# Weights' sums by ScalarE copies and adding DMAs instead of GpSimd, a triple's tiles four apart, and SBUF additions of a triple in two pairs

## The chip, the cores and the metric

The kernel runs on one core of one Trainium2 chip. The metric is the device time of one execution in microseconds (us); the numbers to compare are medians of several executions. The profile and the trace come from one further, profiled execution. Engines are named as in the profile: PE (TensorE; PEld is its weight load), DVE (VectorE), ACT (ScalarE), POOL (GpSimd), and SP (SyncE, which only issues DMAs here).

## The reference

A linear attention with a decay per channel (4 batches, 8 heads, 768 tokens, 48 channels per head) feeds a bilinear feed-forward layer. The weights arrive as 64-bit floats, everything else as 32-bit floats.

```python
f = 1.0 / (1.0 + np.exp(-f_logit))
for t in range(S):
    state = f[:, :, t, :, None] * state + np.einsum('bhd,bhe->bhde', k[:, :, t], v[:, :, t])
    y[:, :, t] = np.einsum('bhd,bhde->bhe', q[:, :, t], state)
...
x = y.transpose(0, 2, 1, 3).reshape(B * S, H * D)      # 3072 x 384
out = (x @ w_a) * (x @ w_b) @ w_out                    # d_ff 1536, out 3072 x 384
```

## The kernel before

All work is in `by_quotients`. Tokens come in 8 blocks of 384 (`BLK`), two to a batch. The attention of a block is two units of four heads each, so there are 16 units (0 to 15). A unit's work is cut into pieces: `front` (two sigmoids on ACT, L284 and L286, one POOL operation, L288, then on DVE two decay scans at L293, L294, eight scans at L303 and two multiplications by q and k at L305 and L306), `scores` (PE L340, DVE L356), `turn` (transposes on PE L368, an ACT copy L372), `gains` (PE L388, DVE L402, L404 and L411), `within` (PE L422) and `across` (PE L443, ACT copies y at L456, and SP moves y into xT, the transposed input of the feed-forward layer).

The feed-forward layer of a block has two halves, "up" (x times w_a and w_b, and their product) and "down" (times w_out).

- Batch 0 (blocks 0 and 1) uses `up` (L490): for one of twelve column tiles of 128, three matmuls for w_b and three for w_a, then an ACT copy (L505) and a DVE multiplication (L507). While these run, the weights are still being converted from 64-bit pieces (`from_double`: ACT at L54, L55, L58 and L59, POOL at L56, DVE at L64 and L66). The raw pieces lie in four places of a pool called `raw`.
- Batches 1 to 3 (blocks 2 to 7) use `up_triples` (L580 to L661). It multiplies a 3x3 arrangement of weight tiles with a 3x2 arrangement of x tiles by fifteen products of sums instead of eighteen plain products; one triple makes three column tiles for both weights, so a block has four triples and the kernel 24. One product is four matmul records at L586. The products are written in a fixed order into four PSUM banks, called v, u, r and t. ACT copies a bank to SBUF (`first` at L617, `late` at L620, L597 in `finish`), and DVE adds: SBUF to SBUF at L621 after a `late` copy, PSUM to SBUF at L624 (`add`). A product may start when the bank's last reader has finished. `finish` (L595 to L601) does the fifteenth product, v6, of a triple inside the next one, then one DVE multiplication of 1152 elements. A triple yields three times.
- `combine_w_ba` (L516 to L549) makes the sums of the weights that the triples need. It has 26 POOL additions at L543 of 128x512 each. Their results lie in the four places of `raw` and partly in w_ba itself.
- `combine_x` (L551 to L578) makes a block's sums of x with 11 DVE operations at L561. It is called ahead of each of blocks 2 to 7, after part 4 of the `down` before it.
- `down` (L680 to L741) takes a pair of 128-token groups and does seven products (x0, m1, x1, m0, x0, m0, x1) of twelve matmuls at L698 each, in two of the four PSUM banks; x0 and x1 are halves of one bank, m0 and m1 of another. Ahead of them DVE makes the sums s3, s1, s2 and s4 (L693), and behind them u2, u3 and the four quarters of the result (L693 too); ACT copies u2 (L711), u3 (L720) and c11 (L733). There are three `down`s in a batch. `combine_w_out` (L667 to L678) makes their weight sums once, in batch 0.

The order of instructions on each engine is the order in which the program writes them. A main list (`rest`) has the ups, triples and downs; beside them runs a queue of (due step, generator) pairs that `beside()` empties. A step is one `up` or a third of a triple; each of the seven parts of a `down` counts half a step. The slots of attention units stand in this queue with due steps written out by hand, and so does `combine_w_ba`:

```python
for_w = combine_w_ba()
queue += [(15.6 + 0.9 * n, for_w) for n in range(9)] + [(24.2 + 0.9 * n, for_w) for n in range(5)]
```

Of the kernel before, what the change touches and what calls it, by code (L numbers as in the profile page):

```python
# [129 lines left out]
def by_quotients(ctx, tc, q, k, f_logit, v, moe_w_a, moe_w_b, moe_w_out, out, ident, weights, bad):  # L130
# [20 lines left out]
    raw_pool = ctx.enter_context(tc.tile_pool(name="raw", bufs=4))  # L151
# [29 lines left out]
    last = groups[:, NTG + 1:2 * NTG].rearrange("p g c -> p (g c)")  # L181
    x_sums = fixed([128, 5 * (BLK // 2)], "x_sums")
    b_copies = itertools.cycle([x_sums[:, BLK * i:BLK * i + BLK] for i in range(2)])
    tails = fixed([128, NU], "tails")
    held = fixed([128, NU, 2], "held")

# [35 lines left out]
    def load_weights(n=1):  # L222
        for _ in range(n):
            if len(raws) == len(todo):
                return
            dst, src, (k, m) = todo[len(raws)]
            raw = dst
            if src.dtype != FP32:

                if len(raws) in EARLY:  # L230
                    raw = groups[:, EARLY.index(len(raws))].bitcast(mybir.dt.uint64)
                else:
                    raw = raw_pool.tile([128, PIECE], mybir.dt.uint64, tag="raw", name="raw")
# [281 lines left out]

    def combine_w_ba():  # L516

        halves = []
        for _ in range(4):
            raw = raw_pool.tile([128, PIECE], mybir.dt.uint64, tag="raw", name="raw").bitcast(FP32)  # L520
            halves += [raw[:, 512 * i:512 * i + 512].rearrange("p (j c) -> p j c", c=128) for i in range(3)]
        s = [halves[2 * i:2 * i + 2] for i in range(6)]
        (a11, a12, a13), (a21, a22, a23), (a31, a32, a33) = (
            [[w_ba[:, g, k].rearrange("p (j i c) -> p i j c", i=NI, c=128)[:, i] for g in range(2)] for k in range(NKT)]
            for i in range(NI)
        )
        for to, x, y, op in (
            (s[0], a21, a32, ALU.add),
            (s[1], a12, a22, ALU.add),
            (s[2], s[1], a21, ALU.add),  # L530
            (s[1], s[1], a23, ALU.add),
            (s[3], a12, s[1], ALU.subtract),
            (s[3], s[3], a32, ALU.subtract),
            (s[4], a31, a11, ALU.subtract),
            (s[5], s[4], a32, ALU.add),
            (s[4], a33, s[4], ALU.subtract),
            (a22, s[1], s[4], ALU.subtract),
            (a22, a22, a13, ALU.add),
            (a31, a31, a33, ALU.subtract),
            (a31, a31, a21, ALU.add),  # L540
        ):
            for g in range(2):
                nc.gpsimd.tensor_tensor(to[g], x[g], y[g], op)  # L543
            yield
        sums_of_w.update(
            v1=s[0], v2=a32, v3=s[3], v4=s[1], v5=a12, v6=s[2],
            u1=a21, u2=a31, u3=s[4], u4=a11, u5=s[5],
            t1=a22, t2=a13, r2=a23, r3=a33,
        )  # L549

    def combine_x(blk):  # L551

        x = xT[blk].rearrange("p k (i t) -> p k i t", i=2)
        (b11, b12), (b21, b22), (b31, b32) = ([x[:, k, i] for i in range(2)] for k in range(NKT))
        s = x_sums.rearrange("p (n t) -> p n t", t=HT)
        more = last[:, 2 * NI * BLK:].rearrange("p (n t) -> p n t", t=HT)
        u5, u3, v6, v1, u1 = (s[:, n] for n in range(5))
        v2, v4, t2, r2 = (more[:, n] for n in range(4))

        def op(to, x, y, op):  # L560
            nc.vector.tensor_tensor(to, x, y, op)  # L561
# [12 lines left out]
        sums_of_x[blk] = dict(  # L574
            v1=v1, v2=v2, v3=b22, v4=v4, v5=b21, v6=v6,
            u1=u1, u2=b12, u3=u3, u4=b11, u5=u5,
            t1=b31, t2=t2, r2=r2, r3=b32,
        )  # L578

    def up_triples(blk):  # L580
# [3 lines left out]
        def times(ps, name, j, start=False):  # L584
            for g in range(2):
                nc.tensor.matmul(  # L586
                    ps[:, g],
                    lhsT=sums_of_w[name][g][:, j],
                    rhs=sums_of_x[blk][name],
                    start=start and g == 0,  # L590
                    stop=True,
# [3 lines left out]
        def finish(j, c, out, v):  # L595
# [2 lines left out]
            a, b = (  # L598
                c[:, g].rearrange("p k i t -> p k (i t)").rearrange("p k (g t) -> p g k t", g=NTG) for g in range(2)
            )  # L600
            nc.vector.tensor_tensor(to[:, :, NI * j:NI * j + NI], a, b, ALU.mult)  # L601

        for j in range(NJ3):
            v, u, r, t = (ps_f[i][:, 0:BLK].rearrange("p (g t) -> p g t", g=2) for i in free)
            free[:] = [free[i] for i in (2, 3, 1, 0)]
            c = (sums, last[:, 0:2 * NI * BLK])[j % 2].rearrange("p (g k i t) -> p g k i t", g=2, k=NI, i=2)
            out = {(k, i): c[:, :, k, i] for k in range(NI) for i in range(2)}
            if j % 2:
                at = (thirds.index(down_first[0]) + 1) * 2
                places = [(at + n) % 6 for n in range(4)]  # L610
                spaces = sums
            else:
                places, spaces = range(4), last
            temps = [spaces[:, BLK * n:BLK * n + BLK].rearrange("p (g t) -> p g t", g=2) for n in places]

            def first(k, i, ps):
                nc.scalar.copy(out[k, i], ps)  # L617

            def late(k, i, ps, temp):
                nc.scalar.copy(temp, ps)  # L620
                nc.vector.tensor_tensor(out[k, i], out[k, i], temp, ALU.add)  # L621

            def add(k, i, ps):
                nc.vector.tensor_tensor(out[k, i], ps, out[k, i], ALU.add)  # L624

            times(v, "v1", j, True)
            first(2, 0, v)
            if tail:
                finish(*tail)
            times(u, "u1", j, True)  # L630
            first(1, 1, u)
            times(r, "r2", j, True)
            add(1, 1, r)
            times(v, "v2", j)
            first(2, 1, v)
# [12 lines left out]
            late(0, 1, v, temps[1])  # L648
            yield
            times(u, "u4", j)  # L650
            late(0, 0, u, temps[2])
            times(t, "t2", j)
            add(0, 1, t)
            times(v, "v5", j)
            late(0, 0, v, temps[3])
            times(u, "u5", j)
            add(2, 0, u)
            tail = j, c, out, v
            if j == NJ3 - 1:
                finish(*tail)  # L660
# [3 lines left out]
    combos = []  # L664
    down_first = [thirds[0]]

    def combine_w_out():  # L667

        b11, b12, b21, b22 = (
            w_out[:, HFT * i:HFT * i + HFT, HM * j:HM * j + HM] for i in range(2) for j in range(2)  # L670
        )
        combos.extend(spare.rearrange("p (i k m) -> i p k m", i=3, k=HFT))
        t1, t2, t4 = combos
        combos.insert(2, b12)
        nc.vector.tensor_tensor(t1, b12, b11, ALU.subtract)
# [3 lines left out]

    def down(pair):  # L680

        b11, b21, b22 = (w_out[:, HFT * i:HFT * i + HFT, HM * j:HM * j + HM] for i, j in ((0, 0), (1, 0), (1, 1)))
        t1, t2, t3, t4 = combos
        (blk0, g0), (blk1, g1) = pair
        a11, a12 = (products(blk0)[:, g0, HFT * i:HFT * i + HFT] for i in range(2))
        a21, a22 = (products(blk1)[:, g1, HFT * i:HFT * i + HFT] for i in range(2))

        def block():
            down_first[0] = thirds[(thirds.index(down_first[0]) + 1) % 3]
            return thirds[thirds.index(down_first[0]) - 1].rearrange("p (k t) -> p k t", k=HFT)  # L690

        def add(to, x, y, op=ALU.add):
            nc.vector.tensor_tensor(to, x, y, op)  # L693
# [2 lines left out]
        def times(to, x, w, first=False):  # L696
            for i in range(HFT):
                nc.tensor.matmul(  # L698
                    to, lhsT=x[:, i], rhs=w[:, i], start=first and i == 0, stop=i == HFT - 1, skip_group_check=True
                )  # L700

        s3 = add(block(), a21, a11, ALU.subtract)
# [89 lines left out]
    with tc.manual_schedule():  # L792
# [540 lines left out]
```

## Time and profile before

| | before |
|---|---|
| median of 3 executions | 634.61 us (632.54 to 634.79) |
| the profiled execution: time | 633.08 us |
| its span in the profile | 631.0 us |
| mean granted PE clock | 0.975 |
| PE busy | 577.4 us (91%) |
| DVE busy | 432.0 us (68%) |
| ACT busy | 276.4 us (44%) |
| POOL busy | 106.0 us (17%) |

The span is what the profile covers; the execution's own time is 2.1 us longer. Busy rows of the page are shares in forty equal slices of the span, 15.8 us each, as a digit in tenths. In the timeline a row is start, duration, engine, line, operation, tiles, and in brackets how long the engine was idle before and what released it. A row of the waits is the waiting instruction, the one waited for, and the total, the number and the longest wait.

The phases of the span are: up to 146 us loading, weight conversion, the attention units of batch 0 and the 24 `up`s; 146 to 219 us the three `down`s of batch 0 with attention units of batch 1; from 219 us blocks 2 to 7 with their triples, and the `down`s of batches 1 to 3 in between.

### The profile page before, as it was taken

The numbers are of one execution on the slowest core, as the hardware profiler recorded it, in microseconds if no ns is written. First come the engines' busy times: TensorE is split into PE (matmuls) and PEld (weight loads), VectorE is DVE, ScalarE is ACT, GpSimd is POOL, SyncE is SP. The second block draws the span as 40 slices with busy tenths as digits, with TensorE's granted clock in tenths as the row PEclk, the third lists the DMA queues.
The fourth block names the chain that finished last, engine by engine and source line by source line (L and its number), as shares of the span: only waits on it lengthen the run. The fifth ranks groups of instructions, "written<-read, shape, count | busy, mean of one in ns | idle before, by whom it ended". The sixth has DMA issues, their size and how long they took to land.

```text
span 631.0 us, 13984 instructions
## 1 busy us (share of the span) xinstructions
PE 577.4 (91%) x5778; PEld 516.0 (82%) x5778; DVE 432.0 (68%) x806; ACT 276.4 (44%) x520; POOL 106.0 (17%) x84
## 2 busy tenths in 40 slices
PE   0769899996899899999999999999999999999995
PEld 0636555554799798899899999899899999999995
DVE  6777345699978677876787667877685556656741
ACT  6577499721133356524552155425541255235400
POOL 6243154897600000000000000000000000000000
PEclk9869999997899899999999999999999999999998
DMA  9886874000024230304030303003000100000000
GB/s 232 242 256 174 193 262 158 2 1 1 1 78 122 69 93 20 77 15 108 1 95 15 108 27 83 13 21 99 3 20 27 45 1 20 2 27 1 1 26 31
DMA packets 30345, 43.66 MB, mean 69 GB/s; under 512 B 3776, under 2 KB 24896, under 8 KB 30272
## 3 DMA queue, kind: packets, MB, share of 16 engines
q1 hardware_dynamic: 29984, 42.38, 24.4%
q8 instruction: 47, 0.77, 0.5%
q10 hardware_dynamic: 288, 0.30, 0.2%
q14 instruction: 26, 0.21, 0.1%
HBM read 33.23 MB, written 4.72 MB: 60 GB/s over the span
## 4 chain that ended last, share of the span: by engine, by line
PE 57%; DVE 6%; ACT 3%; issue 1%; ACTq 0%; DVEq 0%
PE ps_f L586 32%; PE ps_f L698 20%; DVE inv L303 2%; PE ps_y L422 1%; PE ps_x L340 1%; PE ps_y L443 1%; PE ps_x L368 1%; PE ps_x L388 1%; ACT inv L284 1%; DVE sums L621 1%; ACT groups L620 1%; DVE sums L693 1%; DVE k_in L306 1%; ACT f_in L286 1%; DVE q_in L305 1%
## 5 line engine op out<-in xcount | busy, mean ns | idle before, releaser
L490 PE MATMUL ps_f<-xT,w_ba 128*128 128x384 f32 x288 | 97.7, 499 | 7.5 <-DVE w_ba L66 4.6
L586 PE MATMUL ps_f<-xT,w_ba 128*128 128x192 f32 x480 | 95.1, 327 | 0.0
L490 PEld LDWEIGHTS ps_f<-xT,w_ba 128*128 128x128 f32 x288 | 55.0, 194 | 47.6 <-issue 5.8
L586 PEld LDWEIGHTS ps_f<-xT,w_ba 128*128 128x128 f32 x480 | 80.3, 190 | 0.4
L586 PE MATMUL ps_f<-x_sums,raw 128*128 128x192 f32 x384 | 73.9, 330 | 3.9 <-ACT sums L620 3.9
L586 PEld LDWEIGHTS ps_f<-x_sums,raw 128*128 128x128 f32 x384 | 63.3, 190 | 6.6 <-ACT sums L620 6.2
L288 POOL TENSOR_SCALAR inv<-inv 128x768 f32<-128x768 f32 x14 | 13.3, 953 | 275.2 <-ACT inv L284 273.4
L586 PE MATMUL ps_f<-groups,w_ba 128*128 128x192 f32 x288 | 55.4, 329 | 0.1
L698 PE MATMUL ps_f<-spare,sums 128*128 128x192 f32 x288 | 51.2, 335 | 4.5 <-DVE sums L693 3.4
L698 PE MATMUL ps_f<-w_out,sums 128*128 128x192 f32 x288 | 53.2, 336 | 0.0
L698 PEld LDWEIGHTS ps_f<-spare,sums 128*128 128x128 f32 x288 | 48.3, 195 | 5.7 <-DVE sums L693 3.0
L698 PE MATMUL ps_f<-w_out,groups 128*128 128x192 f32 x288 | 52.2, 332 | 0.0
L617 ACT COPY sums<-ps_f 128x384 f32<-128x384 f32 x60 | 28.7, 479 | 47.4 <-PE ps_f L586 47.0
L586 PEld LDWEIGHTS ps_f<-groups,w_ba 128*128 128x128 f32 x288 | 47.8, 190 | 2.0 <-DVE sums L624 1.9
L56 POOL TENSOR_SCALAR sums<-sums 128x768 f32<-128x768 f32 (+1 forms) x20 | 41.0, 2050 | 48.1 <-ACT sums L54 46.3
L698 PEld LDWEIGHTS ps_f<-w_out,groups 128*128 128x128 f32 x288 | 48.6, 194 | 0.2
L698 PEld LDWEIGHTS ps_f<-w_out,sums 128*128 128x128 f32 x288 | 48.2, 195 | 0.7
L617 ACT COPY groups<-ps_f 128x384 f32<-128x384 f32 x60 | 28.7, 478 | 33.4 <-PE ps_f L586 32.0
L620 ACT COPY groups<-ps_f 128x384 f32<-128x384 f32 x60 | 28.7, 478 | 25.5 <-PE ps_f L586 24.4
L621 DVE TENSOR_TENSOR sums<-sums,groups 128x384 f32<-128x384 f32 x48 | 26.6, 555 | 18.9 <-ACT groups L620 18.4
L620 ACT COPY sums<-ps_f 128x384 f32<-128x384 f32 x60 | 28.1, 478 | 20.7 <-PE ps_f L586 20.7
L340 PE MATMUL ps_x<-q_in,k_in 48*64 48x64 f32 x672 | 14.6, 235 | 24.3 <-DVE start L298 15.4
(131 smaller groups left out, 943.8 us busy)
## 6 DMA issues: line engine op xcount, KB each, us to landing
q_in<-in_q_dram SPq DMA_DIRECT2D x32, 144.0 KB, 4.1
k_in<-in_k_dram SPq DMA_DIRECT2D x32, 144.0 KB, 3.5
v_in<-in_v_dram SPq DMA_DIRECT2D x16, 288.0 KB, 4.8
raw<-in_moe_w_out_dram SPq DMA_DIRECT2D x6, 768.0 KB, 4.3
out_dram<-o SPq DMA_DIRECT2D x24, 192.0 KB, 1.9
f_in<-in_f_logit_dram SPq DMA_DIRECT2D x28, 144.0 KB, 3.0
xT<-y SPq DMA_DIRECT2D x46, 72.0 KB, 2.2
raw<-in_moe_w_b_dram SPq DMA_DIRECT2D x4, 768.0 KB, 7.3
```

The lines of the kernel that those rows point to most:

```text
L56: nc.gpsimd.tensor_scalar(h, h, HI_MAX, None, ALU.min)
L284: nc.scalar.activation(inv, x, AF.Sigmoid, bias=less, scale=-1.0, accum_out=tails[:, u:u + 1])
L286: nc.scalar.activation(x, x, AF.Sigmoid)
L288: nc.gpsimd.tensor_scalar(inv, inv, EXP_K, 1.0, ALU.mult, ALU.add)
L303: nc.vector.tensor_tensor_scan(inv[:, w], inv[:, w], none[:, 0:C], first, ALU.mult, ALU.add)
L340: nc.tensor.matmul(ps[h][SUB * p:SUB * p + SUB, o:o + SUB], lhsT=kf[r, tokens(n, c, p)], rhs=qf[r, tokens(n, c, p)], start=True, stop=True,)
L490: nc.tensor.matmul(ps[nm][:, 0:BLK], lhsT=w[:, kt, ft * 128:ft * 128 + 128], rhs=x[:, kt], start=kt == 0, stop=kt == NKT - 1,)
L586: nc.tensor.matmul(ps[:, g], lhsT=sums_of_w[name][g][:, j], rhs=sums_of_x[blk][name], start=start and g == 0, stop=True, skip_group_check= ...
L617: nc.scalar.copy(out[k, i], ps)
L620: nc.scalar.copy(temp, ps)
L621: nc.vector.tensor_tensor(out[k, i], out[k, i], temp, ALU.add)
L698: nc.tensor.matmul(to, lhsT=x[:, i], rhs=w[:, i], start=first and i == 0, stop=i == HFT - 1, skip_group_check=True)
```

## The change

Three parts.

First, `combine_w_ba` makes the sums differently. ACT copies six tiles of 128x1024 (with sign 1 or -1) into the four places of `raw`, which is now one fixed tile; eleven DMAs issued by GpSimd with `accum_op=add` add further weight tiles to them, 512 KB each; four DVE operations of 128x1024 make the last sums in w_ba's own place. Two sums (u2 and u3) change places, and the sign of one changes. The due steps are now half a step apart for the copies and DMAs (from 16.2), and 1.2 for the DVE operations (from 25).

Second, the three column tiles that a triple makes lie four apart in the result instead of next to each other, so that a weight tile row of a triple is 512 adjacent columns; `finish` writes with a stride, and `down` takes its halves as `half_of` picks them.

Third, in a triple the four `late` additions (each a copy to SBUF and a 128x384 addition) become two pairs: two copies, then one addition of 128x768. The product t1 is no longer copied but added from PSUM; t2 goes from the third last to the last place of the order. For v3, `combine_x` has to turn the sign of b22 with an ACT copy of 128x192.

```diff
     def combine_w_ba():
...
+        for to, sign, x in (
+            (s[1], 1, a12), (s[0], 1, a21), (s[3], 1, a22), (s[4], -1, a33), (s[5], -1, a11), (s[2], 1, a12)
+        ):
+            nc.scalar.activation(to, x, AF.Copy, scale=float(sign))
+            yield
+        for to, x in (
+            (s[1], a22), (s[0], a32), (s[3], a23), (s[4], a31), (s[5], a31), (s[2], a22),
+            (s[1], a23), (s[3], a32), (s[4], a21), (s[5], a32), (s[2], a21),
+        ):
+            nc.gpsimd.dma_start(out=to, in_=x, accum_op=ALU.add)
+            yield
+        for to, x, y, op in (
+            (a31, a11, a31, ALU.subtract),
+            (a31, a31, a33, ALU.add),
+            (a22, s[1], a31, ALU.subtract),
+            (a22, a22, a13, ALU.add),
+        ):
+            nc.vector.tensor_tensor(to, x, y, op)
+            yield
...
         op(b21, b21, b22, ALU.subtract)
+        nc.scalar.activation(b22, b22, AF.Copy, scale=-1.0)
...
-            nc.vector.tensor_tensor(to[:, :, NI * j:NI * j + NI], a, b, ALU.mult)
+            nc.vector.tensor_tensor(to.rearrange("p g (k j) t -> p j g k t", k=NI)[:, j], a, b, ALU.mult)
...
-            free[:] = [free[i] for i in (2, 3, 1, 0)]
+            free[:] = [free[i] for i in (2, 1, 3, 0)]
...
             times(u, "u2", j)
-            late(2, 1, u, out[1, 0])
+            copy(first[:, :, 1], u)
             yield
             times(t, "t1", j, True)
-            first(0, 0, t)
             times(v, "v3", j)
-            late(1, 1, v, temps[0])
+            copy(first[:, :, 0], v)
+            nc.vector.tensor_tensor(c[:, :, 1:3, 1], c[:, :, 1:3, 1], first, ALU.add)
             times(u, "u3", j)
-            first(0, 1, u)
+            copy(out[0, 1], u)
             times(r, "r3", j, True)
             add(2, 1, r)
             times(v, "v4", j)
-            late(0, 1, v, temps[1])
+            copy(second[:, :, 1], v)
             yield
             times(u, "u4", j)
-            late(0, 0, u, temps[2])
+            copy(out[0, 0], u)
+            add(0, 0, t)
+            times(v, "v5", j)
+            copy(second[:, :, 0], v)
+            nc.vector.tensor_tensor(c[:, :, 0], c[:, :, 0], second, ALU.add)
+            times(u, "u5", j)
+            add(2, 0, u)
             times(t, "t2", j)
             add(0, 1, t)
-            times(v, "v5", j)
-            late(0, 0, v, temps[3])
-            times(u, "u5", j)
-            add(2, 0, u)
...
+    def half_of(x, i):
+
+        return x.rearrange("p (k j) c -> p k j c", k=NI)[:, :, 2 * i:2 * i + 2]
...
-        queue += [(15.6 + 0.9 * n, for_w) for n in range(9)] + [(24.2 + 0.9 * n, for_w) for n in range(5)]
+        queue += [(16.2 + 0.5 * n, for_w) for n in range(17)] + [(25 + 1.2 * n, for_w) for n in range(5)]
```

More of the change, by code (lines that the diff above doesn't have):

```diff
@@ L150, in by_quotients @@
     sb3 = ctx.enter_context(tc.tile_pool(name="sb3", bufs=3))
-    raw_pool = ctx.enter_context(tc.tile_pool(name="raw", bufs=4))
     ps_a = ctx.enter_context(tc.tile_pool(name="ps_a", bufs=1, space=bass.MemoryType.PSUM))
@@ L183, in by_quotients @@
     b_copies = itertools.cycle([x_sums[:, BLK * i:BLK * i + BLK] for i in range(2)])
+    raws4 = fixedp.tile([128, 4 * PIECE], mybir.dt.uint64, tag="raw", name="raw")
+    raw_places = itertools.cycle([raws4[:, PIECE * i:PIECE * i + PIECE] for i in range(4)])
     tails = fixed([128, NU], "tails")
@@ L232, in load_weights @@
                 else:
-                    raw = raw_pool.tile([128, PIECE], mybir.dt.uint64, tag="raw", name="raw")
+                    raw = next(raw_places)
                 raw = raw[:, 0:k * m].rearrange("p (k m) -> p k m", k=k)
@@ L516, in combine_w_ba @@
     def combine_w_ba():
[L518 to L522, printed above, removed]
+        raw = raws4.bitcast(FP32)
+        s = [raw[:, 1024 * i:1024 * i + 1024].rearrange("p (g c) -> p g c", g=2) for i in range(6)]
         (a11, a12, a13), (a21, a22, a23), (a31, a32, a33) = (
-            [[w_ba[:, g, k].rearrange("p (j i c) -> p i j c", i=NI, c=128)[:, i] for g in range(2)] for k in range(NKT)]
-            for i in range(NI)
-        )
@@ L527, in combine_w_ba @@
[L527 to L544, printed above, removed]
+            [w_ba[:, :, k, 512 * i:512 * i + 512] for k in range(NKT)] for i in range(NI)
+        )
@@ L545, in combine_w_ba @@
         sums_of_w.update(
             v1=s[0], v2=a32, v3=s[3], v4=s[1], v5=a12, v6=s[2],
-            u1=a21, u2=a31, u3=s[4], u4=a11, u5=s[5],
+            u1=a21, u2=s[4], u3=a31, u4=a11, u5=s[5],
             t1=a22, t2=a13, r2=a23, r3=a33,
         )
+        for to, sign, x in (
[9 more added lines that the diff above has]
+            yield
@@ L587, in times @@
                     ps[:, g],
-                    lhsT=sums_of_w[name][g][:, j],
+                    lhsT=sums_of_w[name][:, g, 128 * j:128 * j + 128],
                     rhs=sums_of_x[blk][name],
@@ L608, in up_triples, with copy @@
             if j % 2:
-                at = (thirds.index(down_first[0]) + 1) * 2
-                places = [(at + n) % 6 for n in range(4)]
-                spaces = sums
-            else:
[L613 to L621, printed above, removed]
+                at = thirds.index(down_first[0])
+                pairs = [thirds[(at + n) % 3] for n in (1, 2)]
+            else:
+                pairs = [last[:, PIECE * n:PIECE * n + PIECE] for n in range(2)]
+            first, second = (x.rearrange("p (g n t) -> p g n t", g=2, n=2) for x in pairs)
+            def copy(to, ps):
+                nc.scalar.copy(to, ps)
             def add(k, i, ps):
@@ L626, in up_triples @@
             times(v, "v1", j, True)
-            first(2, 0, v)
+            copy(out[2, 0], v)
             if tail:
@@ L630, in up_triples @@
             times(u, "u1", j, True)
-            first(1, 1, u)
+            copy(out[1, 1], u)
             times(r, "r2", j, True)
@@ L634, in up_triples @@
             times(v, "v2", j)
-            first(2, 1, v)
+            copy(out[2, 1], v)
             times(u, "u2", j)
-            late(2, 1, u, out[1, 0])
+            copy(first[:, :, 1], u)
             yield
             times(t, "t1", j, True)
-            first(0, 0, t)
             times(v, "v3", j)
-            late(1, 1, v, temps[0])
+            copy(first[:, :, 0], v)
+            nc.vector.tensor_tensor(c[:, :, 1:3, 1], c[:, :, 1:3, 1], first, ALU.add)
             times(u, "u3", j)
-            first(0, 1, u)
+            copy(out[0, 1], u)
             times(r, "r3", j, True)
@@ L665, in by_quotients @@
     down_first = [thirds[0]]
+    def half_of(x, i):
+        return x.rearrange("p (k j) c -> p k j c", k=NI)[:, :, 2 * i:2 * i + 2]
     def combine_w_out():
[L669 to L672, printed above, removed]
+        b11, b12, b21, b22 = (half_of(w_out[:, :, HM * j:HM * j + HM], i) for i in range(2) for j in range(2))
+        combos.extend(spare.rearrange("p (i k j m) -> i p k j m", i=3, k=NI, j=2))
         t1, t2, t4 = combos
@@ L680, in down @@
     def down(pair):
-        b11, b21, b22 = (w_out[:, HFT * i:HFT * i + HFT, HM * j:HM * j + HM] for i, j in ((0, 0), (1, 0), (1, 1)))
+        b11, b21, b22 = (half_of(w_out[:, :, HM * j:HM * j + HM], i) for i, j in ((0, 0), (1, 0), (1, 1)))
         t1, t2, t3, t4 = combos
         (blk0, g0), (blk1, g1) = pair
-        a11, a12 = (products(blk0)[:, g0, HFT * i:HFT * i + HFT] for i in range(2))
-        a21, a22 = (products(blk1)[:, g1, HFT * i:HFT * i + HFT] for i in range(2))
+        a11, a12 = (half_of(products(blk0)[:, g0], i) for i in range(2))
+        a21, a22 = (half_of(products(blk1)[:, g1], i) for i in range(2))
         def block():
             down_first[0] = thirds[(thirds.index(down_first[0]) + 1) % 3]
-            return thirds[thirds.index(down_first[0]) - 1].rearrange("p (k t) -> p k t", k=HFT)
+            return thirds[thirds.index(down_first[0]) - 1].rearrange("p (k j t) -> p k j t", k=NI, j=2)
         def add(to, x, y, op=ALU.add):
@@ L698, in times @@
                 nc.tensor.matmul(
-                    to, lhsT=x[:, i], rhs=w[:, i], start=first and i == 0, stop=i == HFT - 1, skip_group_check=True
+                    to, lhsT=x[:, i // 2, i % 2], rhs=w[:, i // 2, i % 2], start=first and i == 0, stop=i == HFT - 1, skip_group_check=True
                 )
```

## The prediction

> **What bounds the kernel now.** I read the page first: PE is busy 577.4 of 631.0 us, and the 40 slices (15.8 us each) show where it is not.
>
> ```profile
> PE   0769899996899899999999999999999999999995
> ...
> POOL 6243154897600000000000000000000000000000
> PEclk9869999997899899999999999999999999999998
> ```
>
> After slice 10, PE is full and POOL empty. The dip in slices 9 and 10 (142 to 174 us) falls on POOL's last busy stretch, with a lowered clock. The table by stretch says the same (columns: busy time and instructions per engine, then clock, DMA share, GB/s):
>
> ```profile
> 145.70:174.60 28.90, 20.18 (x189) 19.11 (x187) 26.25 (x37) 5.32 (x11) 18.56 (x14) 0.82 0.01 4
> 174.60:190.20 15.60, 15.60 (x263) 15.02 (x262) 12.32 (x28) 3.72 (x8) 0.58 (x1) 1.00 0.32 86
> ```
>
> The first row holds the first `down` of batch 0. PE idles 8.7 of 28.9 us there, DVE is full, and the DMA share is 0.01. Next, the waits between 120 and 219 us:
>
> ```profile
> PE ps_x L340 <- DVE k_in L306: 8.9, 2, 5.9
> ...
> PE ps_f L698 <- DVE sums L693: 2.8, 1, 2.8
> ```
>
> PE waits for DVE at 151.93 (5.88 us) and 163.06 (2.84 us); the other 3.0 us of the first line lie at 210.06 and have another cause. The DVE timeline says why DVE is late: the same scans at 147 and at 169 us.
>
> ```profile
> 147.41 2.75 DVE L303 TENSOR_TENSOR_SCAN inv<-inv,start,zero 128x128 f32<-128x128 f32 x2
> ...
> 169.53 0.83 DVE L303 TENSOR_TENSOR_SCAN inv<-inv,start,zero 128x128 f32<-128x128 f32 x2
> ```
>
> Between them POOL's additions (L543) end at 167.3. So to 174 us the bound is DVE, slowed beside POOL; after that it is PE, which in the triples hangs on how soon ACT and DVE empty four PSUM banks:
>
> ```profile
> PE ps_f L586 <- ACT sums L620: 3.9, 5, 0.8
> ...
> PE ps_f L586 <- DVE sums L624: 2.2, 5, 0.5
> ```
>
> These small waits of 219 to 601 us show that the triples have no slack where ACT or DVE has attention work.
>
> [...] The trace has clock 0.82 in the stretch, and twelve L698 matmuls right after the 5.88 us idle take 3.51 instead of 2.11 us. [...] The trace of before has no adding transfer.
>
> **A: the weights' sums.** Removed: 26 POOL additions, 1.3 to 1.9 us each. Added: 6 ACT copies, 11 GpSimd-issued adding DMAs, 4 DVE additions of 128x1024.
>
> What DVE regains: natural rates come from after 169 us (scan 0.40, L293 pair 1.80, 768-element additions 0.95). Then L678 frees L507 before 136.1, the 0.41 us that PE waited there go, and the last `up` ends at 145.65. The scan pair, L294, eight L303 scans and L305/L306 end near 145.6 as well (137.5 + 1.8 + 0.1, the L507 at 141.3, 2.5, 1.8), so the 5.88 us wait goes. From 145.65 PE runs scores 0.72, turn 0.65, gains 0.70 and seven products of 1.95 (two at 2.05 behind attention work): 15.9, so 161.5. DVE is late next: L507 150 us, s1 150.8, s2 151.8, s4 152.8, the first new addition to 154.0, gains to 155.8, u2 156.2. The second x0 waits 0.45 us for u2; other small waits I put at 0.35. L422 starts at 162.3 instead of 174.60. Behind `down` 2's s4 the other two additions cost its second half 0.5. Gain **11.8 us**; 12.5 with no new waits, 9 if a third of DVE's slowness stays.
>
> The four DVE additions: 1.21 us each (1152 elements take 1.36 at L601); the second and fourth lie where DVE waits for PE. If that cover were gone, 1.2 each. The ACT copies are not in the trace; [...] 768 elements take 0.84 at L286, so 0.84 to 1.1; [...]. Two to a step of 3.87, behind the last conversions (120 to 129 us), where ACT idles 3 us a step: nothing; [...].
>
> The DMAs move 512 KB each. [...] below, no less than the 2.2 us that a 72 KB `xT<-y` takes; above, nothing in the trace limits it. [...] The engines stand idle (share 0.01), so they collide with nothing. SP's queue keeps its order and its waits (four places of `raw` as before). On POOL's queue only L289 (L288 of before) lies among them: the third waits behind `front` 4's, at about 130.5. The first DVE addition, at 152.8, needs the fifth. One after another from 121.5, five fit if each takes no more than 6.2 us; the eleventh is needed after 205. [...]
>
> **B1, places.** The tiles of a triple lie four apart: same instructions and sizes, strides inside. Nothing; below nothing has no mechanism, above 0.1 for each of 24 L601.
>
> **B2, additions in pairs.** A triple has 10 ACT copies for 11 and 5 PSUM additions for 4. Two 768-element additions (0.95) replace four of 0.555, so DVE saves 0.3 and pays 0.55 for the new PSUM addition: even. But between v4 and v5, and between u4 and u5, stands one product instead of two or more, and t2, now last, waits for add(0,0,t) behind u4's copy. From the timeline of a quiet triple (560 to 571): matmuls start at T, the ACT copy runs T+0.85 to T+1.33, release +0.05; the weight load of the product after next would start at T+1.14. So v5 waits 0.24, of which 0.09 is won back by faster following loads (0.61 for 0.65): 0.15 remains. Where attention work is put at the second yield, behind v4's copy, it is worse:
> - nine quiet triples x 0.15 = 1.4
> - five with L303 scans: add(0,0,t) stands behind them on DVE, t2 behind that: 0.13 x 5 = 0.7
> - five with L284/L286 (1.9 us of ACT): u4's copy comes 1.98 us late, before as well (1.09 lost then, 239.22), but the next user of its bank is now one product nearer: 1.70, so 0.61 to 0.63 more x 5 = 3.1
> - two with L305/L306 0.1, two with gains 0.27, one with turn 0.2: 0.9
>
> **6.0 us**; 3 if half the waits lie in those of before, 10 if each quiet triple loses 0.3 and t2 always 0.1.
>
> **B3, the negation.** `combine_x` ends with an ACT copy of b22, 0.32 us (L711's size). It waits for the last L561, which still reads b22, and stands on ACT before c11's copy (L733). c11's copy releases the bank that the last product x1 writes. Before, c11 was copied at 357.48 and x1's load began at 359.07, while L561 ended at 359.42. Now 359.42 + 0.05 + 0.32 + 0.32 + 0.05 = 360.15: 1.05 lost. So in five of six (0.97, 1.05, 1.00, 1.05, 1.05); the sixth (217.07) has its L561 done before. **5.1 us**; 0 if DVE ran 1 us ahead, 5.5 at most.
>
> **Sum.** -11.8 + 6.0 + 5.1 = -0.7. On the profiled execution: span 631.0 - 0.7 = 630.3, time 633.08 - 0.7 = 632.4. The median of the runs is 634.61, 1.5 above that execution: **633.9**.
>
> **Rivals.** (1) *The triples swallow the new waits.* For it: waits at L586 exist already, and overlapping ones don't add. Against: PE is full in the quiet triples. 634.6 - 11.8 + 3 + 4.5 = 630.3; with the negation hidden too, 626. (2) *Slower: adding DMAs are slow.* Place: the first DVE addition, behind which `down` 1's gains and u2 stand; it decides from 6.2 us each. At 8 us the fifth lands at 161.5, 9 late: 643. At 10 the eleventh lands at 231.5, 25 later than the first triple would need it: 659. For it: no trace shows one. Against: the engines are idle [...]. (3) *The relief is partial*: [...] half the gain is gone, 639.8. Against: eleven issues replace 43 us of POOL work.
>
> **How the numbers follow.** About 0.5% (3.2 us) is what a measurement can tell from no change: 631.4 and 637.8. Forecast 0.48, own range 629 to 639 (0.2 / 0.6 / 0.2 of it faster, same, slower); rival 1 0.25 (three quarters faster); rival 2 0.15, all slower; rival 3 0.12 (three quarters slower). Faster 0.10 + 0.19 = 0.29, slower 0.10 + 0.15 + 0.09 = 0.34, same 0.37. The range 626.5 to 644 leaves out the tail of rival 2 and of rival 1.
>
> **What would show it.** A right: scans of 0.40 at 140 us, L422 near 162, clock near 1.0 there, [...]. B2 right: waits PE L586 <- ACT copy, 0.15 to 0.24 in each triple, and 1.7 at L284/L286. B3 right: the last product of five downs held by c11's copy, 1 us each. Wrong: DVE waiting for a DMA semaphore between 150 and 215 us, or triples still 9.75 us apart.

## The result, and the profile after

| | before | changed |
|---|---|---|
| median of 20 executions | 634.5 us (632.54 to 636.21) | 636.0 us (633.82 to 637.54) |
| ratio, 95% interval | | 1.002 (1.0008 to 1.0031) |
| the profiled execution: time, span | 633.08, 631.0 us | 636.59, 634.9 us |

The forecast was 0.7 us less. It is 1.3 us more (0.002 x 634.5; 0.5 to 2.0 by the interval): inside the forecast range, and within the 0.5% that was the likeliest case, but on the other side of zero. The page of the changed kernel has these rows:

```profile
PE   0759899999997999998999999998999999999995
...
POOL 6244154552000000000000000000000000000000
PEclk9959999999998999999999999999999999999998
```

The dip of slices 9 and 10 is gone. A new one is in slice 12, and among the 9s of the triples there are two 8s where before there were none. The table by stretch (start:end and length, busy time of PE, PEld, DVE, ACT, POOL with their instructions, then clock, DMA share, GB/s) is cut at the same events as before: last `up`, first L423, second L423, first triple. L423 is the L422 of before.

```profile
147.10:163.80 16.70, 16.42 (x187) 15.56 (x186) 15.18 (x31) 1.76 (x4) 2.66 (x3) 1.00 0.89 151
163.80:180.20 16.40, 16.04 (x267) 15.05 (x268) 15.41 (x32) 5.06 (x10) 0.82 (x1) 1.00 0.36 98
180.20:210.80 30.60, 27.20 (x469) 25.79 (x469) 21.82 (x49) 9.41 (x18) 1.67 (x2) 0.89 0.32 81
```

The first `down` takes 16.7 us instead of 28.6, with the clock at 1.00. DVE's scans show why. This pair takes 0.84 us, where such a pair took 2.75 us before:

```profile
140.35 0.84 DVE L304 TENSOR_TENSOR_SCAN inv<-inv,start,zero 128x128 f32<-128x128 f32 x2
```

The waits of PE's weight loads from 219 us on (waiting, waited for: total, times, longest), first before:

```profile
PEld ps_f L586 <- ACT sums L620: 6.2, 9, 1.1
PEld ps_f L586 <- DVE sums L624: 5.8, 12, 0.7
```

Then the changed kernel:

```profile
PEld ps_f L586 <- ACT groups L616: 9.9, 15, 1.5
PEld ps_f L586 <- DVE sums L619: 6.4, 6, 1.2
PEld ps_f L697 <- ACT o L732: 4.7, 5, 1.0
PEld ps_f L586 <- ACT sums L616: 3.0, 13, 0.4
```

At L586 that is 19.3 us instead of 12.0; the third line, the wait for c11's copy, is new.

To compare by stage, one cuts each profile at events that both kernels have. Two profiles of before and three of the changed kernel (the unchanged kernels profiled again, below) give:

| stage, us | before | changed | difference | forecast |
|---|---|---|---|---|
| start to the last wait of an `up` for x | 72.8, 75.4 | 74.6, 74.1, 74.7 | none to be told | 0 |
| from there to the last `up` | 73.2, 73.4 | 72.6, 72.6, 72.6 | -0.75 | -0.4 |
| first `down`, to L422 | 28.55, 28.53 | 16.72, 16.72, 16.73 | -11.8 | -11.9 |
| second `down`, to L422 | 15.61, 15.61 | 16.32, 16.32, 16.31 | +0.7 | +0.5 |
| third `down`, to the first triple | 28.91, 28.91 | 30.69, 30.18, 30.39 | +1.5 | 0 |
| triples and `down`s, to the last L586 | 377.88, 377.89 | 388.93, 388.99, 388.96 | +11.1 | +11.1 |
| from there to the end | 34.05, 34.27 | 35.10, 34.90, 34.88 | +0.8 | 0 |

The differences sum to +1.5, against a forecast of -0.7. The two large terms met the forecast. It missed in two stages that it had counted at nothing, the third `down` (+1.5) and the end (+0.8).

### The profile page after: what moved, and what is told of

Its sections match the earlier page's. It is cut to its first block, busy times and chain, and to the rows that moved or that the text cites. A ratio compares the mean times of both kernels' runs of the same rounds, so it can differ in the third digit from the quotient of the medians.

```text
span 634.9 us, 13922 instructions
## 1 busy us (share of the span) xinstructions
PE 579.7 (91%) x5778; PEld 512.9 (81%) x5778; DVE 413.6 (65%) x762; ACT 273.6 (43%) x508; POOL 77.0 (12%) x69
## 4 chain that ended last, share of the span: by engine, by line
PE 52%; DVE 11%; ACT 4%; issue 2%; DVEq 0%; ACTq 0%
PE ps_f L586 32%; PE ps_f L697 15%; DVE inv L304 2%; DVE x_sums L560 1%; DVE sums L692 1%; PE ps_x L341 1%; PE ps_y L423 1%; DVE groups L560 1%; PE ps_x L369 1%; DVE sums L637 1%; DVE sums L619 1%; DVE groups L601 1%; ACT inv L285 1%; DVE xT L560 1%; PE ps_y L444 1%
## 5 line engine op out<-in xcount | busy, mean ns | idle before, releaser
L491 PEld LDWEIGHTS ps_f<-xT,w_ba 128*128 128x128 f32 x288 | 55.3, 195 | 47.7 <-DVE w_ba L66 7.3
L616 ACT COPY sums<-ps_f 128x384 f32<-128x384 f32 x108 | 51.8, 480 | 72.0 <-PE ps_f L586 69.0
L616 ACT COPY groups<-ps_f 128x384 f32<-128x384 f32 x108 | 51.7, 479 | 62.8 <-PE ps_f L586 55.1
L586 PE MATMUL ps_f<-xT,w_ba 128*128 128x192 f32 x384 | 78.6, 333 | 0.0
L586 PEld LDWEIGHTS ps_f<-xT,w_ba 128*128 128x128 f32 x384 | 63.4, 190 | 4.8 <-ACT sums L616 2.4
L586 PE MATMUL ps_f<-x_sums,raw 128*128 128x192 f32 x288 | 57.1, 331 | 6.3 <-ACT groups L616 6.2
L586 PE MATMUL ps_f<-groups,w_ba 128*128 128x192 f32 x288 | 55.3, 328 | 4.6 <-DVE sums L619 4.6
L586 PEld LDWEIGHTS ps_f<-x_sums,raw 128*128 128x128 f32 x288 | 46.6, 190 | 9.5 <-ACT groups L616 8.0
L586 PEld LDWEIGHTS ps_f<-groups,w_ba 128*128 128x128 f32 x288 | 47.8, 190 | 6.4 <-DVE sums L619 6.4
L289 POOL TENSOR_SCALAR inv<-inv 128x768 f32<-128x768 f32 x14 | 13.7, 975 | 298.3 <-ACT inv L285 298.3
L619 DVE TENSOR_TENSOR groups<-ps_f,groups 128x384 f32<-128x384 f32 x60 | 32.2, 552 | 17.6 <-ACT groups L616 16.2
L619 DVE TENSOR_TENSOR sums<-ps_f,sums 128x384 f32<-128x384 f32 x60 | 32.1, 551 | 15.1 <-PE ps_f L586 9.9
L586 PE MATMUL ps_f<-x_sums,w_ba 128*128 128x192 f32 x192 | 39.0, 326 | 0.0
L586 PE MATMUL ps_f<-xT,raw 128*128 128x192 f32 x192 | 39.0, 326 | 0.0
## 6 DMA issues: line engine op xcount, KB each, us to landing
raw<-w_ba POOLq DMA_DIRECT2D x11, 512.0 KB, 10.1
```

Of the source, the lines that this page charges most:

```text
L289: nc.gpsimd.tensor_scalar(inv, inv, EXP_K, 1.0, ALU.mult, ALU.add)
L491: nc.tensor.matmul(ps[nm][:, 0:BLK], lhsT=w[:, kt, ft * 128:ft * 128 + 128], rhs=x[:, kt], start=kt == 0, stop=kt == NKT - 1,)
L586: nc.tensor.matmul(ps[:, g], lhsT=sums_of_w[name][:, g, 128 * j:128 * j + 128], rhs=sums_of_x[blk][name], start=start and g == 0, stop=Tru ...
L616: nc.scalar.copy(to, ps)
```

## The experiments

The stage table suggests that the sums bring what was forecast, that the triples' order and the negation cost what was forecast, and that the balance turns on the third `down`. There are three rivals. The triples may be longer through the new places of the tiles or through the DMA-made sums. The early part or the DMA queue may cost something. Or the gain is not as large as its stage shows.

In this section A is the sums, B1 the places, B2 the triple's order and its additions in pairs, and B3 the negation, as in the prediction. An edit is shown against the changed kernel, if nothing else is said.

**The negation alone undone**: it goes out of `combine_x`, and the weights' sum for v3 is turned at the end of `combine_w_ba` instead.

```diff
-        nc.scalar.activation(b22, b22, AF.Copy, scale=-1.0)
+        nc.scalar.activation(s[3], s[3], AF.Copy, scale=-1.0)
```

> The changed kernel without the ACT negation of b22 that ends combine_x six times; instead the weights' sum for v3 is turned in sign once, by one ACT copy of 128x1024 at the end of combine_w_ba. Theory (the negation holds c11's copy and so the last product of five downs; the changed trace shows 4.73 us of such waits): 636.0 - 4.7 = 631.3 us, and no wait of PE at L697 for the c11 copy is left. Rival (the wait is made good later in the following triple, or the bank would have been held anyway): 635 to 636 us.

631.94 us, ratio to before 0.9959 (0.9944 to 0.9974): 4.1 below the changed kernel, where 4.7 was expected. The triples' stage takes 384.45 us, 4.5 less. The waits of PE's weight loads no longer have a line for c11's copy:

```profile
PEld ps_f L586 <- ACT groups L616: 9.9, 15, 1.5
PEld ps_f L586 <- DVE sums L619: 5.3, 5, 1.2
PEld ps_f L586 <- ACT sums L616: 3.0, 13, 0.4
```

So B3 costs 4.5 us, and the mechanism is the one predicted. In the changed kernel ACT's timeline shows the negation (L573) waiting for DVE with c11's copy (L732) behind it, and PEld's timeline the weight load that this held:

```profile
355.03 0.36 ACT L573 ACTIVATE xT<-xT 128x192 f32<-128x192 f32 x1 [7.50 <-DVE xT L560]
355.30 0.30 ACT L732 COPY o<-ps_f 128x192 f32<-128x192 f32 x1
```

```profile
355.65 1.44 PEld L697 LDWEIGHTS ps_f<-spare,groups 128*128 128x128 f32 x9 [0.97 <-ACT o L732]
```

**The triple's order and additions alone undone**: the loop body of the kernel before in the changed one, everything else as changed.

```diff
-            free[:] = [free[i] for i in (2, 1, 3, 0)]
+            free[:] = [free[i] for i in (2, 3, 1, 0)]
...
             times(t, "t1", j, True)
+            first(0, 0, t)
...
             times(u, "u4", j)
-            copy(out[0, 0], u)
-            add(0, 0, t)
+            late(0, 0, u, temps[2])
+            times(t, "t2", j)
+            add(0, 1, t)
             times(v, "v5", j)
-            copy(second[:, :, 0], v)
-            nc.vector.tensor_tensor(c[:, :, 0], c[:, :, 0], second, ALU.add)
+            late(0, 0, v, temps[3])
             times(u, "u5", j)
             add(2, 0, u)
-            times(t, "t2", j)
-            add(0, 1, t)
```

> The changed kernel with the triple's order, copies and additions of the kernel before (four single SBUF additions, t1 copied, t2 third from the end); weights' sums, places and negation stay as changed. Theory (one product between two uses of a bank costs 7.4 us more of waits at L586 than before, 19.5 against 12.0): 636.0 - 7.5 = 628.5 us. Rival (the triples are longer for another reason, such as weight tiles that lie in 512 adjacent columns or strided writes): 634 to 636 us.

627.41 us, ratio 0.9878 (0.9853 to 0.9903), 8.6 below the changed kernel. The triples' stage is 382.38 us, 6.6 less than changed, where 7.5 was expected. Of the rest, 1.1 us lies in the third `down` (29.34 us) and 0.7 at the end; neither belongs to the triples.

**Both undone**: sums and places are all that is left of the change.

> Both undone at once: old triples, and the sign turned once in the weights. What is left of the change is the weights' sums by copies and adding DMAs, and the places four apart. Theory (the three costs add up; the sums bring 8.3 us up to the first triple in the traces, and 11.8 by the forecast): 623 to 626 us, that is 12.2 below the changed kernel. Rival (costs overlap, so that either edit alone hides the other): 628 us or more.

621.77 us, ratio 0.9820 (0.9797 to 0.9843), somewhat below the 623 to 626 us expected. The triples' stage takes 377.76 us, against 377.88 before. So the places (B1) and the DMA-made sums cost the triples nothing, and B2 (6.6) and B3 (4.5) add up to the 11.1. The rival of overlapping costs falls. A and B1 together are worth 12.7 us by the medians (10 to 13 by the interval); in its profile no half clock followed the wait in the third `down`, on which see below.

**The sums on POOL again**, at their old due steps and without the copies and the DVE additions; the rest is as changed (the sign of v3's sum as the new triples want it).

```diff
-            nc.gpsimd.dma_start(out=to, in_=x, accum_op=ALU.add)
...
+            for g in range(2):
+                nc.gpsimd.tensor_tensor(to[:, g], x[:, g], y[:, g], op)
```

> The changed kernel with the weights' sums made by 26 POOL additions again, at the old due steps; new triples and negation stay. Theory: the whole give-back without the gain, 634.5 + 12.2 = 646.7 us. Rival (part of the give-back comes from the adding DMAs, through clock or through loads that they delay): 640 to 643 us.

645.18 us, ratio 1.0171 (1.0157 to 1.0185), between the 646.7 expected and the rival's 640 to 643. The stages decide: the triples take 389.15 us, as with the DMAs, and the first `down` 28.63, as before. The cost of B without A is the same 11 us, so none of it comes from the DMAs.

**Pairs kept, the old order restored.** The sign is turned once, too. t2 stands between u4 and v5 again, t1 is copied, and u4 is added from PSUM by DVE instead of copied by ACT.

```diff
-            free[:] = [free[i] for i in (2, 1, 3, 0)]
+            free[:] = [free[i] for i in (2, 3, 1, 0)]
...
             times(t, "t1", j, True)
+            copy(out[0, 0], t)
...
-            copy(out[0, 0], u)
-            add(0, 0, t)
+            add(0, 0, u)
+            times(t, "t2", j)
+            add(0, 1, t)
             times(v, "v5", j)
...
-            times(t, "t2", j)
-            add(0, 1, t)
```

> The kernel with the sign turned once, and in the triple the pairs of SBUF additions kept, but the old spacing: t1 is copied again, u4 is added from PSUM, t2 stands between u4 and v5 again (10 ACT copies, 5 PSUM additions and 2 pair additions, as in the changed triple). Theory (it is the single product between two uses of a bank that costs, not the pairs): at least as fast as the old triples, 621.8 us or less; about 617 if u4 on DVE also takes away the 1.09 us waits behind the two sigmoids. Rival (the longer pair additions hold DVE and so the banks): near 631.9 us, as with the changed triples.

623.03 us, ratio 0.9811 (0.9790 to 0.9831). The triples' stage is 374.86 us: 9.6 less than with the changed order (384.45), 2.9 less than with old triples (377.76). The waits at L586 on ACT are nearly gone. u4's bank is now released by DVE and not by an ACT copy behind two sigmoids:

```profile
PEld ps_f L586 <- DVE sums L619: 7.5, 6, 1.4
...
PEld ps_f L586 <- ACT sums L616: 1.8, 6, 0.4
```

So it is not the pairs as such that cost. Nor is it u4's copy on ACT alone, since the old triples have this copy too and don't pay the 6.6 us. That leaves the changed order, with a single product between two uses of a bank, as the likely cause. It is not shown alone, since this run changes u4's release as well; how the gain of 2.9 us divides between the pairs and this release is open, too. The whole time missed the 621.8 us or less that was expected: in its profile the third `down` took 30.35 us and the end 35.47, against 27.66 and 34.03 with both undone.

**The third `down`.** In every kernel above, PE waits for k_in before the third scores, first before, then changed:

```profile
210.06 1.25 PE L340 MATMUL ps_x<-q_in,k_in 48*64 48x64 f32 x48 [3.03 <-DVE k_in L306]
200.36 1.65 PE L341 MATMUL ps_x<-q_in,k_in 48*64 48x64 f32 x48 [3.24 <-DVE k_in L307]
```

After this wait PE runs at half clock for 0, 3.4 or 6.8 us (sums_alone, before, changed). In the traces the clock changes at steps of 3.41 us: in the changed kernel its stretches last 13.65, 153.60, 6.83 and 423.25 us, which are 4, 45, 2 and 124 steps. In the three profiles of this kernel the wait begins 0.5, 1.5 and 1.1 us after such a step. The table by stretch, cut at these steps, shows first the changed kernel, then the one with both undone (its clock does not change here, so the steps are counted on from its last change, at 45.56 us), then before. PE's busy time is the first after the comma, the clock third from last.

```profile
196.65:200.07 3.42, 0.46 (x35) 0.31 (x24) 3.39 (x9) 0.36 (x1) 0.00 (x0) 1.00 0.52 104
200.07:203.48 3.41, 3.12 (x53) 3.01 (x54) 1.66 (x3) 2.08 (x4) 0.83 (x1) 0.50 0.00 0
203.48:206.89 3.41, 3.41 (x14) 3.32 (x13) 1.75 (x4) 0.00 (x0) 0.00 (x0) 0.50 0.02 5
```

```profile
195.75:199.16 3.41, 1.59 (x53) 1.21 (x51) 3.32 (x11) 0.00 (x0) 0.00 (x0) 1.00 0.83 178
199.16:202.57 3.41, 1.98 (x54) 1.92 (x55) 2.29 (x4) 1.92 (x4) 0.83 (x1) 1.00 0.03 7
```

```profile
207.28:210.69 3.41, 0.63 (x37) 0.63 (x41) 2.69 (x6) 0.60 (x1) 0.00 (x0) 1.00 0.25 60
210.69:214.11 3.42, 3.42 (x34) 3.30 (x25) 2.72 (x4) 1.48 (x4) 0.83 (x1) 0.50 0.02 5
```

In the first and the third fence a window in which PE is busy for only 0.46 or 0.63 us is followed by half clock. In the second a step cuts the wait near its middle, PE is busy for 1.59 and 1.98 us in the two windows, and no half clock follows. So the window ahead of a half clock need not be wholly idle. How idle, these runs do not show: by the records of the matmuls, windows of this stage idle for 0.51 and 0.53 of their length (neg_once, sums_alone) had no half clock behind them, windows idle for 0.53 and 0.55 (old_triple, after_2) had.

Whether one or two follow goes with where the wait ends. In the three profiles of the changed kernel and in spaced_pairs it ran 0.3 to 1.4 us past the step at which the clock fell, and two windows at half clock followed. In old_triple and in the four profiles with the sums on POOL (late_dma's among them) it ended before that step, and one followed.

Over the seven profiles with the new sums and this wait the stage took 27.7 us (two, no half clock), 29.3 (one window) and 30.2 to 30.7 (four, two windows), 29.5 on average; over the four with the sums on POOL always 28.9 to 29.0. So A's 11.9 us in the stages before come with a lottery here. On the average of these seven it costs 0.6 us against before, and it cost 1.5 in the three profiles of the changed kernel.

Two runs remove the wait: `combine_x` of batch 0 goes behind the attention work that is due at the same part.

```diff
-                if part == 4 and rest[n + 1:] and rest[n + 1][0] is up_triples:
+                if part == 4 and rest[n + 1:] and rest[n + 1][0] is up_triples and blk:
                     combine_x(rest[n + 1][1])
                 step += 0.5
                 if part != 3:
                     beside()
+                if part == 4 and rest[n + 1:] and rest[n + 1][0] is up_triples and not blk:
+                    combine_x(rest[n + 1][1])
```

With old triples and the sign turned once (both undone, as above):

> The kernel with old triples and the sign turned once, but in batch 0 combine_x comes after the attention work that is due at the same part of the third down. Theory (the wait of 3.24 us for k_in before the third down's scores costs itself and, by lot, 1.7 or 3.4 us of half clock): no such wait, the stretch from the second L422 to the first triple 25 to 26 us instead of 27.7 to 30.7, and 621.8 - 2.5 = 619.3 us or less. Rival (combine_x then holds the first triple instead): 621 to 622 us.

617.97 us, ratio 0.9743 (0.9731 to 0.9756), 3.8 below the same kernel with the wait. The stage takes 24.13 us instead of 27.66, without wait or half clock:

```profile
195.78 0.89 PE L423 MATMUL ps_y<-at,v_in 64*48 64x64 f32 x48
196.48 0.92 PE L341 MATMUL ps_x<-q_in,k_in 48*64 48x64 f32 x48
197.33 2.22 PE L700 MATMUL ps_f<-w_out,sums 128*128 128x192 f32 x12
```

In the changed kernel:

> The changed kernel, with nothing but combine_x of batch 0 put behind the attention work that is due at the same part of the third down. Theory (the wait of 3.24 us before the third down's scores stays in the changed kernel and brings it, by lot, none, one or two half-clock windows of 3.4 us, 1.5 us of time on average): second L422 to first triple 24 to 25 us instead of 30.7, and 636.0 - 3.5 - 1.5 = 631.0 us. Rival (no half clock on average, only the wait): 632.5 us. Rival (what the sums gave is lost elsewhere): 635 us or more.

634.79 us, ratio 1.0004 (0.9993 to 1.0014). The 631.0 and 632.5 us expected were missed; the time is next to that of the last rival, 635 or more, but for a reason that it did not name. The stage still takes 29.86 us, because the negation stands on ACT ahead of the copy of kT (L373) and waits for `combine_x`, which is now late:

```profile
204.52 0.36 ACT L573 ACTIVATE xT<-xT 128x192 f32<-128x192 f32 x1 [5.63 <-DVE xT L560]
204.79 0.30 ACT L732 COPY o<-ps_f 128x192 f32<-128x192 f32 x1
204.99 0.80 ACT L373 COPY kT<-ps_x 128x768 f32<-128x768 f32 x1
```

```profile
205.84 1.13 PE L389 MATMUL ps_x<-v_in,kT 64*48 64x48 f32 x40 [4.22 <-ACT kT L373]
```

One wait took the place of the other, and one window at half clock followed it. The negation, where it stands, takes away what the later `combine_x` gains.

**An adding DMA at the end of the kernel before** (the edit is against before).

```diff
+            if (blk, i) == (B - 1, (even[0], odd[0])):
+                nc.gpsimd.dma_start(out=sums_of_w["v1"][0].rearrange("p j c -> p (j c)"), in_=w_ba[:, 0, 0, 0:512], accum_op=ALU.add)
```

> The kernel before with one GpSimd-issued adding DMA of 256 KB after the last triple, whose result nobody reads. Every kernel with adding DMAs so far reached the matmul at 73 us (the last wait for x in the ups) at 74.0 to 74.9 us, the two without at 72.8 and 73.1. Theory (a program with a software DMA queue starts 1.5 us later): 74.5 us there, 636 us in all. Rival (loads and clock differ from execution to execution): 72.5 to 75 us there, 634.5 us in all.

635.56 us, ratio 1.0011 (1.0002 to 1.0019), and 74.9 us to the last wait for x. The expectation's rival holds for the early part, since the second profile of before had 75.4 there without any such DMA. That the whole is 0.7 us longer is at the edge of what was measured, and its cause is open. It may be part of the changed kernel's time as well.

**The unchanged kernels profiled again**, before once and the changed one twice; their stages are in the table above.

> The kernel before once more, for a second profile. Theory (stages of a kernel repeat to 0.1 us, apart from loads and half-clock windows): 72.9 us to the last wait for x, 28.55 us for the first down, 15.6 for the second, 377.9 for the triples; the third down 27.2, 28.9 or 30.6 with no, one or two half-clock windows of 3.4 us. Rival (the early 1.5 us is execution noise): 74 us or more to the last wait for x.

635.96 us in that one execution: 3.0 us more span than the first profile, 2.6 of them before the last wait for x, so the rival of scatter between executions holds.

> The changed kernel once more, for the spread of its stages. Theory: 72.6 us from the last wait for x to the last up, 16.7 for the first down, 16.3 for the second, 388.9 for the triples, and 27.7, 29.3 or 30.7 from the second L422 to the first triple with no, one or two half-clock windows. Rival: this last stretch is always 30.7.

635.45 us. The stages held, except that the third `down` was 30.18.

> The changed kernel again, a third profile: the same numbers are expected as for the second one, with a stretch from the second L422 to the first triple of 27.7, 29.3 or 30.7 us.

636.30 us, third `down` 30.39. All three profiles of the changed kernel have two half-clock windows. That fits the rival (this stage is always long), though other kernels with the same work up to there drew none and one. Whether chance or something in this kernel decides it is open.

**All that helped, together** (new sums, places, sign turned once, pairs with old spacing, `combine_x` of batch 0 later).

> All that helped put together: weights' sums by copies and adding DMAs, places four apart, sign turned once, pairs with the old spacing, combine_x of batch 0 behind the attention work. Theory (the pairs with spacing save 2.9 us in the triples' stretch against the old triples, and this adds to the 618.0 us of the kernel with old triples): 615 us. Rival (spacing gains were execution noise, as the whole of spaced_pairs at 623.0 against 621.8 suggests): 618 us.

615.71 us, ratio 0.9707 (0.9689 to 0.9724): 18.8 us below before. The triples' stage takes 374.85 us, the third `down` 24.12. This is 2.3 us below late_x, which has old triples. So without the wait the gain of the pairs with u4's new release shows in the whole time, too.

## Why the prediction was right or wrong

**A, right.** For the last `up` and two `down`s 11.8 us were forecast and 11.9 measured (0.75 + 11.8 - 0.7). The scans run at 0.42 us each, the clock is 1.00, and L423 came 16.7 us after the last `up`, as forecast (162.3 - 145.65). The second `down` lost 0.7 us for 0.5; its u2 comes behind a DVE addition of 1.22 us.

**The adding DMAs, right in effect, wrong in size.** The forecast put a price on one transfer, from issue to landing, that was the author's estimate; the trace of before has no adding transfer to show it. It was too low. The profile page of the changed kernel has

```profile
raw<-w_ba POOLq DMA_DIRECT2D x11, 512.0 KB, 10.1
```

The shortest took 5.4 us and the longest 14.4; the 10.1 is the median. They land one after another: the nine issued from 133 us on land 2.6 to 3.3 us apart, 2.9 on average (138.64 to 161.47 us in the trace). The deciding price was 6.2 us each one after another. The first addition ran at 154.20, right behind s4, and rival 2 did not come. Rival 3 did not either: no scan is slow beside the DMA issues (the pair of L294 at 136.95 took 1.80 us, the price forecast without POOL). ACT's copies cost 1.05 us each, where the forecast had 0.84 to 1.1, and nothing on the path.

**B1, right**: 0.1 us less, nothing.

**B2, right in mechanism, 0.6 too little**: 6.0 us forecast, 6.6 measured (388.96 - 382.38). The quiet triples are 9.94 us apart instead of 9.75, so each loses 0.19 for 0.15: the predicted wait is there, and little of it is won back.

```profile
577.03 0.62 PEld L586 LDWEIGHTS ps_f<-xT,w_ba 128*128 128x128 f32 x4 [0.21 <-ACT sums L616]
```

Behind the sigmoids u5 waited 1.54 us. The forecast was 1.70, and the 0.21 that v5 had waited just before come off it:

```profile
231.25 0.62 PEld L586 LDWEIGHTS ps_f<-x_sums,raw 128*128 128x128 f32 x4 [1.54 <-ACT groups L616]
```

One reading of B2 was wrong. A triple of before has five `late` additions from SBUF (120 at L621 for 24 triples), not four, and the fifth is gone as well. So by the prediction's own prices DVE does not come out even but saves 0.3 us a triple (5 x 0.555 - 2 x 0.95 - 0.55).

**B3, right in mechanism, 0.6 too much**: 5.1 us forecast, 4.5 measured; each of the five waits was 0.91 to 0.97 us instead of 0.97 to 1.05. That the triples' stage met its 11.1 us so closely is luck, since the misses of B2 and B3 cancel.

**The failed step: the third `down` at nothing.** The prediction set aside "the other 3.0 us of the first line", at 210.06, as having "another cause", and summed as if that stage stayed as it was. The wait did stay (3.24 us for 3.03), but not its price. The prediction had seen the clock as part of the loss in the first `down`, and did not ask where against the clock's steps (3.41 us apart in the traces) a wait would come to lie that stays and comes some ten us earlier. In the profiles of the changed kernel it ran across a step, and two windows at half clock followed (6.8 us) instead of one (3.4), and the stage took 1.5 us more.

The end of the kernel is the second term left out. From the end of the last DVE addition to the end of the span it is 6.7 to 6.9 us instead of 5.6 to 5.8. The difference lies among the closing instructions, behind the issue of the last output DMA. It is not shown that the change causes it: after_late_x, which ends with the same instructions, has 6.1 us there, spaced_pairs 7.3. The cause stays open.

With terms of 11.8 and 11.1 against each other, these two, 2.3 together, decided the sign; the third `down` alone turns -0.7 into +0.8.

Rival 1 (the triples swallow the waits) fell: undone one by one, B2 and B3 give back 6.6 and 4.5 us, which is the whole 11.1.

## What to carry to other kernels

A change that gains in one stage and pays in another is a bundle: price each part by its own stage and try each alone. Here the sums and places were worth 12.7 us without the other two parts.

A sign that must be turned is best turned once, in the operand that is made once (here the weights' sum). Turned per block on ACT, it waits for that block's sums of x, and every PSUM copy behind it in ACT's order waits with it (4.5 us of the triples' stage here).

In a chain over few PSUM banks, count the products between two uses of a bank. In the quiet triples one was too few for a copy that ends 1.33 us after the product's start (PE's weight load waited 0.21 us), and two were enough.

A wait that a change leaves in place can still change its price (here 3.24 us of wait for 3.03, and a stage 1.5 us longer). Where the clock falls after a wait, ask where the wait will lie, or take it away.

## What the runs showed of the hardware

- 512 KB adding DMAs from SBUF to SBUF, queued, landed 2.9 us apart on average (2.6 to 3.3, changed kernel). Each issue kept POOL 1.2 to 3.2 us (median 1.7).
- While they ran in the changed kernel, DVE's scans (0.42 us) and 768-element additions (0.95) kept their times. The one addition that was slow among them, 1.98 us instead of 1.36, also ran beside a POOL operation (L289). Beside POOL additions of the kernel before, which took 1.3 to 2.4 us each (the prediction has 1.9 as the most), the same scans took up to 3.3 times as long (1.38 us).
- A wait of PE of 3.2 us came with a stage of 27.7 us (sums_alone, no half clock), of 29.3 (old_triple, 3.4 us at half clock) or of 30.2 to 30.7 (the changed kernel and spaced_pairs, 6.8 us), and lay differently against the clock's steps of 3.41 us each time.
